# Eight PSUM banks in one tile and the remainder's steps reordered, in a six-layer cross network

## The chip, the cores and the metric

The kernel runs on one core of one Trainium2 chip. The metric is the device time of one execution in microseconds (us). The core has five engines that work off their own queues in order and wait for each other through semaphores: TensorE (PE in the profile; PEld are its weight loads), VectorE (DVE), ScalarE (ACT), GpSimd (POOL) and SyncE (SP). SP computes nothing here; it issues most of the transfers (DMA). Matmul results land in PSUM, eight banks of 512 fp32 columns by 128 partitions; all else lies in SBUF, 128 partitions wide.

## The reference

```python
B, F, D, L = 4096, 26, 16, 6
Din = min(F * D, 1024)          # 416
# x0: B x Din, ws: L x Din x Din, bs: L x Din, all bfloat16
def reference(x0, ws, bs):
    x = x0
    for l in range(ws.shape[0]):
        x = x0 * (x @ ws[l] + bs[l]) + x
    return x
```

Each of the six layers is a product of a 4096x416 matrix with a 416x416 one, then a bias, an elementwise product with the input, and an elementwise sum.

## The kernel before, in words

**Layout.** For layers 0 to 4, features lie on partitions and the 4096 batch rows on columns. 416 features are three blocks of 128 (k or m = 0, 1, 2) and a remainder of 32. The three blocks are in XM[i], with i = 0 for the input and two more for the running x. The remainder is packed into XR[i]: its 32 features for four groups of 512 batch rows lie one below the other on 128 partitions. The batch is cut into two halves s = 0, 1 of 2048, each into four groups g of 512 columns. The weights are in WM (the 384 main input rows of each layer), WR (the 32 remainder rows, repeated four times down the partitions) and WD (the remainder's own 32x32 block, laid out so that one matmul handles one group).

**Loads.** Eight transposing transfers (load_x0t, L78), all issued by SP, bring the input's main part into XM[0], 512 batch rows at a time. The remainder comes in rows of 64 bytes into xrem[s] (load_xrem, L83); x0_rem(s) then makes the packed layout from it on VectorE: 32x32 block transposes into xrt[s] (L145), a strided copy into XR[0] (L147), and two copies that put the upper 64 partitions into the lower 64 of XRx[s] and the other way round (L149), so that a remainder matmul can use either half of the rows of the array. WR of layer 0 is loaded early; the loads of WR for layers 1 to 5 (load_wr, L86) stand on SP behind the eight input transposes. fill_wd(0, 1) and fill_wd(1, L) copy the remainder blocks from WR to WD on GpSimd (L120); the second call waits for those later loads.

**Layer 0** is first_layer(s), for s = 0 and then s = 1. PE first multiplies the main blocks (function full, L206) for the first 1024 columns and the three output blocks m, into PSUM tiles pa[0] to pa[2]; then come the remainder rows (function row, L213) that close these sums; then pb[0] to pb[2] for the other 1024 columns. ew_main evicts each PSUM tile with ScalarE, which adds the bias (L154), then multiplies with the input (L155) and adds x (L156) on VectorE. The remainder's own output is made by rem_pair (mm_rem, L180 and L185; ew_rem, L160 to L162) after both halves.

**Layers 1 to 4** do the same in tiles of 2048 columns by 128 features (mm_full, L168; mm_row, L174), each in two PSUM tiles of two banks.

**The last layer** turns the product round, so that batch rows lie on partitions and the result needs no transpose: quads q = 0 to 7 of four blocks of 128 rows each, 416 columns per block. Two quads make a round: mm_q_full (L301) for the first two blocks, then mm_q_rows for both quads (remainder L309, bias by a row of ones L313), then the other blocks. ew_pair evicts two blocks at once (L322 to L325). In the last round, six of the eight blocks are evicted one by one by ew_single (L332 to L335); the output of the last block but one is issued from ScalarE's queue.

**Order.** The kernel sets manual_schedule, so each engine runs its instructions in the order in which the program text issues them; tiles from pools add the semaphores. PSUM comes from one pool of four tiles of two banks.

Of the kernel before, what the change touches and what calls it, by code (L numbers as in the profile page):

```python
# [10 lines left out]
ALU = mybir.AluOpType  # L11
# [5 lines left out]
def kernel(  # L17
# [23 lines left out]
    tpool = ctx.enter_context(tc.tile_pool(name="tpool", bufs=4))  # L41
    opool = ctx.enter_context(tc.tile_pool(name="opool", bufs=10))
    psum = ctx.enter_context(tc.tile_pool(name="psum", bufs=4, space=bass.MemoryType.PSUM))
# [37 lines left out]
    def load_xrem(eng, s):  # L81
        with nc.allow_non_contiguous_dma(reason="64B row segments"):
            eng.dma_start(xrem[s][:], x0[SW * s:SW * s + SW, NK * P:D].rearrange("(p t) r -> p t r", t=16))  # L83
# [15 lines left out]
    load_xrem(nc.scalar, 0)  # L99
    nc.scalar.activation(dz[:, 1:2], dz[:, 0:1], ACT.Identity, bias=dz[:, 0:1], scale=1.0)  # L100
    for g in range(1, NG):
        load_x0t(0, g)
        nc.vector.tensor_copy(WR[32 * g:32 * g + 32, 0, :], WR[0:32, 0, :])  # L103
    load_x0t(1, 0)
    load_xrem(nc.sync, 1)
    for g in range(1, NG):
        load_x0t(1, g)
# [17 lines left out]
    wps = psum.tile([P, CW], FP32, tag="ps", name="wps")  # L125

    def pe_filler(n, cols):
        for i in range(n):
            nc.tensor.matmul(wps[:, 0:cols], lhsT=warm[:, 0:P], rhs=warm[:, 0:cols], start=True, stop=True)  # L129
# [4 lines left out]
    def bias_setup():  # L134
        pb = psum.tile([P, 4, 8], BF16, tag="ps", name="pb")
        for m in range(NK):
            nc.tensor.transpose(pb[:, m, 0:L], bsb[0:L, 128 * m:128 * m + 128], ident[0:L, 0:L])
        for g in range(NG):
            nc.tensor.transpose(pb[32 * g:32 * g + 32, 3, 0:L], bsb[0:L, NK * P:D], ident[0:L, 0:L], tile_position=(0, 32 * g))
        nc.vector.tensor_copy(bM[:], pb[:, 0:NK, 0:L])  # L140
        nc.vector.tensor_copy(bR[:], pb[:, 3, 0:L])


    def x0_rem(s):
        nc.vector.transpose(out=xrt[s][:], in_=xrem[s][:])  # L145
        xr = XR[0][:, CW * s:CW * s + CW]
        nc.vector.tensor_copy(xr.rearrange("p (j t) -> p j t", t=16), xrt[s][:].rearrange("p t j -> p j t"))  # L147
        for a in range(2):
            nc.vector.tensor_copy(XRx[s][64 * a:64 * a + 64, :], XR[0][64 - 64 * a:128 - 64 * a, CW * s:CW * s + CW])  # L149

    def ew_main(l, s, m, h, pt, cur, nxt):
        c0 = col0(s, 2 * h)
        t = tpool.tile([P, 2 * CW], BF16, name="t")
        nc.scalar.activation(t[:], pt[:].rearrange("p a b -> p (a b)"), ACT.Identity, bias=bM[:, m, l:l + 1], scale=1.0)  # L154
        nc.vector.tensor_tensor(out=t[:], in0=t[:], in1=XM[0][:, m, c0:c0 + 2 * CW], op=ALU.mult)  # L155
        nc.vector.tensor_tensor(out=nxt[:, m, c0:c0 + 2 * CW], in0=t[:], in1=cur[:, m, c0:c0 + 2 * CW], op=ALU.add)  # L156
# [7 lines left out]
    def mm_full(l, s, m, g, pts, cur, first, last):  # L164
        c0 = col0(s, g)
        for k in range(NK):
            for q in range(4):
                nc.tensor.matmul(pts[g // 2][32 * q:32 * q + 32, g % 2, :], lhsT=WM[:, l, k, 128 * m + 32 * q:128 * m + 32 * q + 32],  # L168
                                 rhs=cur[:, k, c0:c0 + CW], start=(first and k == 0), stop=(last and k == NK - 1),
                                 tile_position=(0, 32 * q))  # L170

    def mm_row(l, s, m, pts, curR, first, last):
        for g in range(NG):
            nc.tensor.matmul(pts[g // 2][:, g % 2, :], lhsT=WR[32 * g:32 * g + 32, l, 128 * m:128 * m + 128],  # L174
                             rhs=curR[32 * g:32 * g + 32, CW * s:CW * s + CW],
                             start=first, stop=last, tile_position=(32 * g, 0))

    def mm_rem(l, s, pr, cur, curR):
        for g in range(NG):
            nc.tensor.matmul(pr[32 * g:32 * g + 32, :], lhsT=WD[:, l, g, :], rhs=curR[:, CW * s:CW * s + CW],  # L180
                             start=True, stop=False, tile_position=(0, 32 * g))
        for k in range(NK):
            for g in range(NG):
                c0 = col0(s, g)
                nc.tensor.matmul(pr[32 * g:32 * g + 32, :], lhsT=WM[:, l, k, NK * P:D], rhs=cur[:, k, c0:c0 + CW],  # L185
                      start=False, stop=(k == NK - 1), tile_position=(0, 32 * g))

    def new_pts():
        return [psum.tile([P, 2, CW], FP32, tag="ps", name=f"pt{h}") for h in range(2)]
# [7 lines left out]
    def first_layer(s):  # L197
        cur, nxt = XM[0], XM[1]

        def new_pt(m):  # L200
            return psum.tile([P, 2, CW], FP32, tag="ps", name=f"ph{m}")

        def full(pt, m, h, gl, first, last):
            c0 = col0(s, 2 * h + gl)
            for k in range(NK):
                nc.tensor.matmul(pt[:, gl, :], lhsT=WM[:, 0, k, 128 * m:128 * m + 128], rhs=cur[:, k, c0:c0 + CW],  # L206
                                 start=(first and k == 0), stop=(last and k == NK - 1))

        def row(pt, m, h, swapped, first):
            for gl in range(2):  # L210
                r0 = 32 * ((2 * h + gl + 2 * swapped) % 4)
                src = XRx[s][r0:r0 + 32, :] if swapped else XR[0][r0:r0 + 32, CW * s:CW * s + CW]
                nc.tensor.matmul(pt[:, gl, :], lhsT=WR[r0:r0 + 32, 0, 128 * m:128 * m + 128], rhs=src,  # L213
                                 start=first, stop=(not first), tile_position=(r0, 0))

        pa = [new_pt(m) for m in range(NK)]
        for gl in range(2):
            for m in range(NK):
                full(pa[m], m, 0, gl, True, False)
        pb = [new_pt(0)]  # L220
        row(pa[0], 0, 0, 0, False)
        row(pa[1], 1, 0, 1, False)
        row(pa[2], 2, 0, 0, False)
        row(pb[0], 0, 1, 0, True)
        for m in range(NK):
            ew_main(0, s, m, 0, pa[m], cur, nxt)
        for gl in range(2):
            full(pb[0], 0, 1, gl, False, True)
        ew_main(0, s, 0, 1, pb[0], cur, nxt)
        for m in range(1, NK):  # L230
            pb.append(new_pt(m))
            for gl in range(2):
                full(pb[m], m, 1, gl, True, False)
        row(pb[1], 1, 1, 0, False)
        row(pb[2], 2, 1, 1, False)
        for m in range(1, NK):
            ew_main(0, s, m, 1, pb[m], cur, nxt)
# [3 lines left out]
    x0_rem(0)  # L241
    first_layer(0)
    x0_rem(1)
    first_layer(1)

    def rem_pair(l, cur, curR, nxtR, feeds_last):
        pr2 = psum.tile([P, 2, CW], FP32, tag="ps", name="pr2")
# [9 lines left out]
    rem_pair(0, XM[0], XR[0], XR[1], False)  # L257
# [40 lines left out]
    def mm_q_full(q, py, gs, first):  # L298
        for g in gs:
            for k in range(NK):  # L300
                nc.tensor.matmul(py[g // 2][:, g % 2, 0:D], lhsT=cur[:, k, q_cols(q, g)], rhs=WM[:, l, k, :],  # L301
                                 start=(first and k == 0), stop=((not first) and k == NK - 1))


    def mm_q_rows(q, pys):
        for a in range(2):
            s, i = quads[q + a]
            for g in range(NG):
                nc.tensor.matmul(pys[a][g // 2][:, g % 2, 0:D], lhsT=curR[32 * g:32 * g + 32, CW * s + 128 * i:CW * s + 128 * i + 128],  # L309
                                 rhs=WR[32 * g:32 * g + 32, l, :], start=(a == 1 or g >= 2), stop=False, tile_position=(32 * g, 0))  # L310
        for a in range(2):
            for g in range(NG):
                nc.tensor.matmul(pys[a][g // 2][:, g % 2, 0:D], lhsT=ones[32 * g:32 * g + 1, :],  # L313
                                 rhs=bLr[32 * g:32 * g + 1, :], start=False, stop=(a == 0 and g < 2), tile_position=(32 * g, 0))
# [12 lines left out]
    def ew_single(q, g, py, eng):  # L327
# [6 lines left out]
        nc.vector.tensor_tensor(out=o[:, 0, :], in0=t[:, 0:D], in1=XLrows[:, b, :], op=ALU.add)  # L334
        return lambda: eng.dma_start(out_v[:, b, :], o[:, 0, :])  # L335

    for q in range(0, NQ, 2):
        last = q + 2 == NQ
# [3 lines left out]
        mm_q_rows(q, py)  # L342
        ew_pair(q, 0, py[0])
        if not last:
            mm_q_full(q, py[0], (2, 3), False)
            ew_pair(q, 1, py[0])
            for h in range(2):
                mm_q_full(q + 1, py[1], (2 * h, 2 * h + 1), False)
                ew_pair(q + 1, h, py[1])
        else:  # L350
            for a, g in ((0, 2), (0, 3), (1, 0), (1, 1), (1, 2), (1, 3)):
                mm_q_full(q + a, py[a], (g,), False)
                ew_single(q + a, g, py[a], nc.scalar if (a, g) == (1, 2) else nc.sync)()
# [30 lines left out]
```

## Time and profile before

| | us |
|---|---|
| median of 3 runs | 137.73 (136.46 to 138.05) |
| the profiled execution | 136.52 |
| its span, first to last instruction | 134.4 |
| PE, DVE, ACT, POOL busy in it | 122.7, 111.0, 83.9, 6.0 |
| mean granted TensorE clock | 0.998 |

The profile describes one execution. Its page gives busy time per engine, the tenths of busy time in 40 slices of the span, the chain of work that ended last, and the costliest groups of instructions. The trace behind it gives each instruction with its start, and for idle time the event that ended it (after the arrow). A line number is that of the kernel's text. "issue" stands for waiting that the profile shows no cause for. A matmul is listed with its whole length, some 380 ns, but matmuls follow each other closer than that, so the pace of PE is read from starts.

The largest groups by time:

```profile
L168 PE MATMUL pt<-XM,WM 128*32 128x512 bf16 x1152 | 65.2, 379 | 0.0
L154 ACT ACTIVATE t<-pt,bM 128x1024 bf16<-128x1024 f32 x48 | 49.6, 1115 | 20.7 <-PE pt L174 20.7
L155 DVE TENSOR_TENSOR t<-t,XM 128x1024 bf16<-128x1024 bf16 x60 | 41.7, 695 | 7.0 <-ACT t L154 7.0
L156 DVE TENSOR_TENSOR XM<-t,XM 128x1024 bf16<-128x1024 bf16 x60 | 41.7, 696 | 3.5
```

### The profile page before, as it was taken

How to read it: one execution, taken by the hardware profiler on the slowest of the kernel's cores; microseconds unless marked ns; L12 is line 12 of the kernel's file. 1: busy time of each engine (PE TensorE's matmuls, PEld its weight loads, DVE VectorE, ACT ScalarE, POOL GpSimd, SP SyncE). 2: the span in 40 equal slices, each digit the busy share in tenths (PEclk: the TensorE clock that was granted, in tenths of full speed). 3: DMA queues.
4: the chain of work that ended last, by engine and by line, in shares of the span. 5: the costliest groups of instructions: out<-in, count | busy, mean ns of one | idle time of the engine just before them, and what ended most of it. 6: DMA issues, size and time to landing. Idle time of an engine off the chain costs nothing.

```text
span 134.4 us, 3926 instructions
## 1 busy us (share of the span) xinstructions
PE 122.7 (91%) x1681; PEld 54.8 (41%) x1683; DVE 111.0 (83%) x194; ACT 83.9 (62%) x91; POOL 6.0 (4%) x18
## 2 busy tenths in 40 slices
PE   6979984998999999999999999999999999999640
PEld 2323331443444444444444434444444444544310
DVE  1254996998897988999898989898989999999852
ACT  1306833883939495859577856849584966766640
POOL 4110000400000000000000000000003200000000
PEclk9999999999999999999999999999999999999999
DMA  3999999999930000000000000000598999965541
GB/s 97 247 225 189 163 228 236 304 330 333 335 97 0 0 5 2 5 0 5 0 5 0 5 0 5 0 5 0 106 133 185 170 203 188 274 222 185 180 147 56
DMA packets 41989, 16.37 MB, mean 122 GB/s; under 512 B 30794, under 2 KB 41972, under 8 KB 41972
## 3 DMA queue, kind: packets, MB, share of 16 engines
q1 hardware_dynamic: 39304, 15.53, 50.9%
q10 hardware_dynamic: 2668, 0.59, 2.3%
q8 instruction: 13, 0.21, 0.6%
q14 instruction: 4, 0.03, 0.1%
HBM read 6.15 MB, written 3.41 MB: 71 GB/s over the span
## 4 chain that ended last, share of the span: by engine, by line
PE 70%; SPq 15%; DVE 5%; DMA 4%; ACT 2%; issue 1%; ACTq 0%
PE pt L168 45%; PE pt L301 12%; SPq L78 12%; PE pt L174 5%; DMA WM<-in_ws_dram 4%; PE pr L185 4%; DVE XM L156 2%; ACT t L332 2%; DVE t L155 1%; PE pt L309 1%; SPq L86 1%; PE pr L180 1%; SPq L74 1%; PE pt L313 1%; DVE t L333 1%
## 5 line engine op out<-in xcount | busy, mean ns | idle before, releaser
L168 PE MATMUL pt<-XM,WM 128*32 128x512 bf16 x1152 | 65.2, 379 | 0.0
L154 ACT ACTIVATE t<-pt,bM 128x1024 bf16<-128x1024 f32 x48 | 49.6, 1115 | 20.7 <-PE pt L174 20.7
L155 DVE TENSOR_TENSOR t<-t,XM 128x1024 bf16<-128x1024 bf16 x60 | 41.7, 695 | 7.0 <-ACT t L154 7.0
L156 DVE TENSOR_TENSOR XM<-t,XM 128x1024 bf16<-128x1024 bf16 x60 | 41.7, 696 | 3.5
L168 PEld LDWEIGHTS <-WM 128*32 128x32 bf16 x1152 | 29.7, 97 | 33.8 <-issue 5.1
L154 ACT ACTIVATE t<-ph,bM 128x1024 bf16<-128x1024 f32 x12 | 12.5, 1113 | 12.5 <-PE ph L213 12.5
L301 PE MATMUL pt<-WM,XM 128*128 128x416 bf16 x96 | 18.2, 339 | 1.8 <-ACT t L332 1.8
L206 PE MATMUL ph<-XM,WM 128*128 128x512 bf16 x70 | 16.3, 379 | 1.2 <-DMA XM<-in_x_dram 1.1
L322 ACT CAST t<-pt 128x832 bf16<-128x832 f32 x13 | 11.1, 852 | 5.8 <-PE pt L313 3.1
L301 PEld LDWEIGHTS <-XM 128*128 128x128 bf16 x96 | 9.0, 98 | 10.8 <-issue 3.9
L206 PEld LDWEIGHTS <-WM 128*128 128x128 bf16 x72 | 6.8, 98 | 10.1 <-issue 2.7
L185 PE MATMUL pr<-XM,WM 128*32 128x512 bf16 x120 | 8.2, 379 | 0.0
L324 DVE TENSOR_TENSOR o<-t,XLrows 128x832 bf16<-128x832 bf16 x13 | 7.7, 592 | 0.6
L323 DVE TENSOR_TENSOR t<-t,X0rows 128x832 bf16<-128x832 bf16 x13 | 7.6, 586 | 0.4 <-ACT t L322 0.3
L174 PE MATMUL pt<-XR,WR 32*128 32x512 bf16 x96 | 7.3, 379 | 0.6 <-DVE XR L162 0.6
L160 ACT ACTIVATE t<-pr,bR 128x512 bf16<-128x512 f32 x10 | 6.3, 686 | 2.1 <-PE pr L185 2.1
L129 PE MATMUL wps<-warm 128*128 128x512 bf16 (+1 forms) x12 | 4.2, 518 | 1.2 <-DVE warm L89 1.2
L254 POOL COPY XLrows<-scrR 128x512 bf16<-128x512 bf16 x2 | 1.7, 891 | 77.5 <-DMA scrR<-XR 77.5
L332 ACT CAST t<-pt 128x416 bf16<-128x416 f32 x6 | 3.0, 506 | 3.0 <-DVE o L334 1.4
L162 DVE TENSOR_TENSOR XR<-t,XR 128x512 bf16<-128x512 bf16 x10 | 4.3, 425 | 0.8
L103 DVE COPY WR<-WR 32x416 bf16<-32x416 bf16 x3 | 0.8, 259 | 4.6 <-DMA WR<-in_ws_dram 4.6
L185 PEld LDWEIGHTS <-WM 128*32 128x32 bf16 x120 | 3.2, 97 | 3.2
(36 smaller groups left out, 38.3 us busy)
## 6 DMA issues: line engine op xcount, KB each, us to landing
X0rows<-in_x_dram SPq DMA_DIRECT2D x4, 832.0 KB, 10.5
out_dram<-o SPq DMA_DIRECT2D x13, 208.0 KB, 2.2
WM<-in_ws_dram SPq DMA_DIRECT2D x5, 312.0 KB
WR<-in_ws_dram SPq DMA_DIRECT2D x4, 130.0 KB, 4.8
out_dram<-o SPq DMA_DIRECT2D x5, 104.0 KB, 1.7
WM<-in_ws_dram ACTq DMA_DIRECT2D x1, 312.0 KB, 3.5
XM<-in_x_dram SPq DMA_TRANSPOSE x8, 4.8
xrem<-in_x_dram ACTq DMA_DIRECT2D x1, 128.0 KB
```

The costliest lines, as they stand in the source:

```text
L78: nc.sync.dma_start_transpose(out=XM[0][:, :, c0:c0 + CW], in_=x0[c0:c0 + CW, 0:NK * P])
L154: nc.scalar.activation(t[:], pt[:].rearrange("p a b -> p (a b)"), ACT.Identity, bias=bM[:, m, l:l + 1], scale=1.0)
L155: nc.vector.tensor_tensor(out=t[:], in0=t[:], in1=XM[0][:, m, c0:c0 + 2 * CW], op=ALU.mult)
L156: nc.vector.tensor_tensor(out=nxt[:, m, c0:c0 + 2 * CW], in0=t[:], in1=cur[:, m, c0:c0 + 2 * CW], op=ALU.add)
L168: nc.tensor.matmul(pts[g // 2][32 * q:32 * q + 32, g % 2, :], lhsT=WM[:, l, k, 128 * m + 32 * q:128 * m + 32 * q + 32], rhs=cur[:, k, c0:c ...
L174: nc.tensor.matmul(pts[g // 2][:, g % 2, :], lhsT=WR[32 * g:32 * g + 32, l, 128 * m:128 * m + 128], rhs=curR[32 * g:32 * g + 32, CW * s:CW ...
L185: nc.tensor.matmul(pr[32 * g:32 * g + 32, :], lhsT=WM[:, l, k, NK * P:D], rhs=cur[:, k, c0:c0 + CW], start=False, stop=(k == NK - 1), tile ...
L206: nc.tensor.matmul(pt[:, gl, :], lhsT=WM[:, 0, k, 128 * m:128 * m + 128], rhs=cur[:, k, c0:c0 + CW], start=(first and k == 0), stop=(last ...
L301: nc.tensor.matmul(py[g // 2][:, g % 2, 0:D], lhsT=cur[:, k, q_cols(q, g)], rhs=WM[:, l, k, :], start=(first and k == 0), stop=((not first ...
L322: nc.scalar.copy(tv, py[h][:, :, 0:D])
L323: nc.vector.tensor_tensor(out=tv, in0=tv, in1=X0rows[:, b0:b0 + 5:4, :], op=ALU.mult)
L324: nc.vector.tensor_tensor(out=o[:], in0=tv, in1=XLrows[:, b0:b0 + 5:4, :], op=ALU.add)
```

## The change

- PSUM is one tile PS of eight banks; two_banks() hands out pairs of banks in turn. The buffers t go from four to six.
- The bias is brought onto partitions by matmuls with the identity into fp32, not by transposes into bf16.
- load_xrem and x0_rem take a range of partitions, and x0_rem an engine for its copies. The first half's remainder is loaded in two parts: partitions 0 to 63 from ScalarE's queue at the head, 64 to 127 from SP ahead of the fourth input transpose. The second half's load moves behind one more transpose.
- x0_rem(0, 0, 64) stays at the head, on VectorE. x0_rem(0, 64, 128) stands in first_layer(0), its block transposes on VectorE and its copies on GpSimd. x0_rem(1) moves into first_layer(0), ahead of the elementwise work on its second 1024 columns.
- In first_layer(0) all remainder rows of pb come after all main products of pb. In first_layer(1) the main products go block by block; the first layer's remainder product (rem_first) comes ahead of the last two evictions of main blocks.
- In the last layer, the last two quads are opened one at a time, all eight of their blocks are evicted singly, the sum of each block is issued after the product of the next, and all outputs go from SP.
- skip_group_check is passed to the matmuls.

```diff
-    tpool = ctx.enter_context(tc.tile_pool(name="tpool", bufs=4))
+    tpool = ctx.enter_context(tc.tile_pool(name="tpool", bufs=6))
     opool = ctx.enter_context(tc.tile_pool(name="opool", bufs=10))
-    psum = ctx.enter_context(tc.tile_pool(name="psum", bufs=4, space=bass.MemoryType.PSUM))
+    psum = ctx.enter_context(tc.tile_pool(name="psum", bufs=1, space=bass.MemoryType.PSUM))
...
-    def load_xrem(eng, s):
+    def load_xrem(eng, s, p0, p1):
         with nc.allow_non_contiguous_dma(reason="64B row segments"):
-            eng.dma_start(xrem[s][:], x0[SW * s:SW * s + SW, NK * P:D].rearrange("(p t) r -> p t r", t=16))
+            eng.dma_start(xrem[s][p0:p1], x0[SW * s + 16 * p0:SW * s + 16 * p1, NK * P:D].rearrange("(p t) r -> p t r", t=16))
...
-    load_xrem(nc.scalar, 0)
+    load_xrem(nc.scalar, 0, 0, 64)
     nc.scalar.activation(dz[:, 1:2], dz[:, 0:1], ACT.Identity, bias=dz[:, 0:1], scale=1.0)
     for g in range(1, NG):
-        load_x0t(0, g)
         nc.vector.tensor_copy(WR[32 * g:32 * g + 32, 0, :], WR[0:32, 0, :])
+    load_x0t(0, 1)
+    load_x0t(0, 2)
+    load_xrem(nc.sync, 0, 64, 128)
+    load_x0t(0, 3)
     load_x0t(1, 0)
-    load_xrem(nc.sync, 1)
-    for g in range(1, NG):
-        load_x0t(1, g)
+    load_x0t(1, 1)
+    load_xrem(nc.sync, 1, 0, 128)
+    load_x0t(1, 2)
+    load_x0t(1, 3)
     load_wm(nc.sync, 1)
     for g in range(NG):
         load_wr(nc.sync, g, 1, L)
...
     fill_wd(0, 1)
     fill_wd(1, L)
...
-    wps = psum.tile([P, CW], FP32, tag="ps", name="wps")
+    PS = psum.tile([P, 8, CW], FP32)
+    turn = [0]
+
+    def two_banks():
+        i = 2 * (turn[0] % 4)
+        turn[0] += 1
+        return PS[:, i:i + 2, :]
...
-        pb = psum.tile([P, 4, 8], BF16, tag="ps", name="pb")
+        pb = PS[:, 7, 0:32].rearrange("p (a b) -> p a b", a=4)
         for m in range(NK):
-            nc.tensor.transpose(pb[:, m, 0:L], bsb[0:L, 128 * m:128 * m + 128], ident[0:L, 0:L])
+            nc.tensor.matmul(pb[:, m, 0:L], lhsT=bsb[0:L, 128 * m:128 * m + 128], rhs=ident[0:L, 0:L], start=True, stop=True,
+                             skip_group_check=True)
...
-    def x0_rem(s):
-        nc.vector.transpose(out=xrt[s][:], in_=xrem[s][:])
-        xr = XR[0][:, CW * s:CW * s + CW]
-        nc.vector.tensor_copy(xr.rearrange("p (j t) -> p j t", t=16), xrt[s][:].rearrange("p t j -> p j t"))
-        for a in range(2):
-            nc.vector.tensor_copy(XRx[s][64 * a:64 * a + 64, :], XR[0][64 - 64 * a:128 - 64 * a, CW * s:CW * s + CW])
+    def x0_rem(s, p0, p1, eng):
+        nc.vector.transpose(out=xrt[s][p0:p1], in_=xrem[s][p0:p1])
+        eng.tensor_copy(XR[0][p0:p1, CW * s:CW * s + CW].rearrange("p (j t) -> p j t", t=16),
+                              xrt[s][p0:p1].rearrange("p t j -> p j t"))
+        for a in range(p0, p1, 64):
+            eng.tensor_copy(XRx[s][64 - a:128 - a, :], XR[0][a:a + 64, CW * s:CW * s + CW])
...
+        pa = [two_banks() for m in range(NK)]
+        if s == 0:
+            for gl in range(2):
+                for m in range(NK):
+                    full(pa[m], m, 0, gl, True, False)
+        else:
             for m in range(NK):
-                full(pa[m], m, 0, gl, True, False)
-        pb = [new_pt(0)]
+                for gl in range(2):
+                    full(pa[m], m, 0, gl, True, False)
+        pb = [two_banks()]
         row(pa[0], 0, 0, 0, False)
         row(pa[1], 1, 0, 1, False)
         row(pa[2], 2, 0, 0, False)
-        row(pb[0], 0, 1, 0, True)
+        if s == 1:
+            row(pb[0], 0, 1, 0, True)
+        if s == 0:
+            x0_rem(0, 64, 128, nc.gpsimd)
         for m in range(NK):
             ew_main(0, s, m, 0, pa[m], cur, nxt)
         for gl in range(2):
-            full(pb[0], 0, 1, gl, False, True)
-        ew_main(0, s, 0, 1, pb[0], cur, nxt)
+            full(pb[0], 0, 1, gl, s == 0, s == 1)
+        if s == 1:
+            ew_main(0, s, 0, 1, pb[0], cur, nxt)
         for m in range(1, NK):
-            pb.append(new_pt(m))
+            pb.append(two_banks())
             for gl in range(2):
                 full(pb[m], m, 1, gl, True, False)
-        row(pb[1], 1, 1, 0, False)
-        row(pb[2], 2, 1, 1, False)
-        for m in range(1, NK):
-            ew_main(0, s, m, 1, pb[m], cur, nxt)
+        if s == 0:
+            row(pb[0], 0, 1, 0, False)
+            row(pb[2], 2, 1, 1, False)
+            row(pb[1], 1, 1, 0, False)
+            x0_rem(1, 0, 128, nc.vector)
+            for m in range(NK):
+                ew_main(0, s, m, 1, pb[m], cur, nxt)
+        else:
+            row(pb[1], 1, 1, 0, False)
+            row(pb[2], 2, 1, 1, False)
+            rem_first(pb)
 
     bias_setup()
     pe_filler(1, CW)
-    x0_rem(0)
-    first_layer(0)
-    x0_rem(1)
-    first_layer(1)
+    x0_rem(0, 0, 64, nc.vector)
...
+    def rem_first(pb):
+        pr2 = two_banks()
+        for s in range(NS):
+            mm_rem(0, s, pr2[:, s, :], XM[0], XR[0])
+        for s in range(NS):
+            ew_rem(0, s, pr2[:, s, :], XR[0], XR[1])
+            ew_main(0, 1, 1 + s, 1, pb[1 + s], XM[0], XM[1])
+
+    first_layer(0)
+    first_layer(1)
...
-    for q in range(0, NQ, 2):
-        last = q + 2 == NQ
+
+        def close():
+            nc.vector.tensor_tensor(out=o[:, 0, :], in0=t[:, 0:D], in1=XLrows[:, b, :], op=ALU.add)
+            nc.sync.dma_start(out_v[:, b, :], o[:, 0, :])
+
+        return close
+
+    for q in range(0, NQ - 2, 2):
         py = [new_pts()]
         mm_q_full(q, py[0], (0, 1), True)
         py.append(new_pts())
-        mm_q_rows(q, py)
+        mm_q_rows((q, q + 1), py, q)
         ew_pair(q, 0, py[0])
-        if not last:
-            mm_q_full(q, py[0], (2, 3), False)
-            ew_pair(q, 1, py[0])
-            for h in range(2):
-                mm_q_full(q + 1, py[1], (2 * h, 2 * h + 1), False)
-                ew_pair(q + 1, h, py[1])
-        else:
-            for a, g in ((0, 2), (0, 3), (1, 0), (1, 1), (1, 2), (1, 3)):
-                mm_q_full(q + a, py[a], (g,), False)
-                ew_single(q + a, g, py[a], nc.scalar if (a, g) == (1, 2) else nc.sync)()
+        mm_q_full(q, py[0], (2, 3), False)
+        ew_pair(q, 1, py[0])
+        for h in range(2):
+            mm_q_full(q + 1, py[1], (2 * h, 2 * h + 1), False)
+            ew_pair(q + 1, h, py[1])
+    pending = []
+    for q in range(NQ - 2, NQ):
+        py = new_pts()
+        mm_q_rows((q,), (py,), None)
+        for g in range(NG):
+            mm_q_full(q, py, (g,), False)
+            close = ew_single(q, g, py)
+            if pending:
+                pending.pop()()
+            pending.append(close)
+    pending.pop()()
...
```

## The prediction

> **What bounds the kernel now.** I read the busy table first, then the chain that ended last, then the table of waits, and then the order of instructions in the first 42 us and the last 12 us. The busy table and the digits of the 40 slices say who carries the time (columns: busy us, share of the span, instructions; then tenths of each slice):
>
> ```profile
> PE 122.7 (91%) x1681; PEld 54.8 (41%) x1683; DVE 111.0 (83%) x194; ACT 83.9 (62%) x91; POOL 6.0 (4%) x18
> ...
> PE   6979984998999999999999999999999999999640
> ```
>
> TensorE (PE) is full from about slice 10 to slice 36. A change can win only in the holes of the first ten slices (0 to 33 us) and in the last four, and any new hole on PE comes straight out as time. GpSimd (POOL) looks free with 4%, and that is the trap to look into. The waits show the holes (us in total, times, longest):
>
> ```profile
> POOL WD L120 <- DMA WR<-in_ws_dram: 20.7, 5, 15.9
> ...
> PE ph L213 <- DVE XR L147: 2.0, 1, 2.0
> ...
> PE pt L301 <- ACT t L332: 1.8, 3, 0.6
> ...
> ACT t L332 <- DVE o L334: 1.4, 1, 1.4
> ...
> PE pt L174 <- DVE XR L162: 0.6, 1, 0.6
> ```
>
> PE waits 2.0 us for the second half's remainder (x0_rem(1), queued on VectorE behind six elementwise pairs), 0.6 us for the first layer's new remainder, and 1.8 us in the last round for ScalarE's evictions. POOL itself waits 20.7 us for the remainder weights of the later layers. Its instructions in order of time (start, length, idle before):
>
> ```profile
> 6.09 1.06 POOL L120 COPY WD<-WR 32x32 bf16<-32x32 bf16 x4 [3.97 <-DMA WR<-in_ws_dram]
> 23.07 0.31 POOL L120 COPY WD<-WR 32x160 bf16<-32x160 bf16 x1 [15.91 <-DMA WR<-in_ws_dram]
> 23.76 0.45 POOL L120 COPY WD<-WR 32x160 bf16<-32x160 bf16 x1 [0.38 <-DMA WR<-in_ws_dram]
> 24.42 0.52 POOL L120 COPY WD<-WR 32x160 bf16<-32x160 bf16 x1 [0.21 <-DMA WR<-in_ws_dram]
> 25.12 0.54 POOL L120 COPY WD<-WR 32x160 bf16<-32x160 bf16 x1 [0.19 <-DMA WR<-in_ws_dram]
> 103.12 1.73 POOL L254 COPY XLrows<-scrR 128x512 bf16<-128x512 bf16 x2 [77.46 <-DMA scrR<-XR]
> ```
>
> From 7.15 to 25.66 us POOL stands at, or works off, the four copies of fill_wd(1, L). They wait for loads that the DMA-issuing engine (SP) starts only at 18.46 us, behind all eight input transposes. Nothing behind those copies in POOL's order can start before 25.66 us.
>
> **The change part by part.**
>
> *The remainder on POOL.* For the first half s = 0, x0_rem is split at partition 64. The lower part stays on VectorE at the head. Of the upper part only the 32x32 transposes stay on VectorE; the strided copy into XR[0] and the copy into XRx[0] go to POOL, and they are issued after fill_wd(1, L). So they stand directly behind the copy that ended at 25.66 us. Who waits: the first-layer rows of pb, whose operand is just that upper half (XR[0] partitions 64 to 127, and XRx[0] partitions 0 to 63). PE reaches these rows where it ran the s = 0 rows before, at 15.36 us:
>
> ```profile
> 1.19 3.83 PE L129 MATMUL wps<-warm 128*128 128x256 bf16 x11 [1.19 <-DVE warm L89]
> ...
> 15.36 0.39 PE L213 MATMUL ph<-XR,WR 32*128 32x512 bf16 x2
> ...
> 15.69 4.06 PE L206 MATMUL ph<-XM,WM 128*128 128x512 bf16 x18
> ```
>
> Behind them on PE's queue stands everything else, the whole second half of the batch included. When are they released? SP has one more issue ahead of the WR loads, the second part of xrem[0]: the whole load took 0.67 us to issue, half of it 0.33 by size (ends: 0, if the loads are paced by the traffic, and 0.67). So the last WD copy ends at 25.66 + 0.33 = 25.99. The trace shows no such copy on POOL; the nearest row is L254, 128x512, 0.72 and 1.06 us, mean 0.89. Two of them, one waiting for the other: 25.99 + 1.78 + two gaps of 0.04 = 27.85. The rows of pb[0] can go after the first copy, at 26.9, the other four at 27.85.
>
> From there PE's work up to the next common point, the rows of layer 1 (L174 at 32.37 before), is, start to start in the timeline of before: four rows 0.33, 18 matmuls 3.99, eight rows 0.55, 18 matmuls 3.99, four rows 0.32, the remainder product 1.74, 48 matmuls of layer 1 2.70. The sum is 13.62, so 27.85 + 13.62 = 41.47, which is 9.10 us later than 32.37. (Before, the same 13.62 from 15.36 and 3.39 us of waiting made 32.37; those waits are swallowed by the long one and are not to be taken off again.) ScalarE's evictions don't lengthen this: pb[0] of s = 0 leaves at 27.3 to 28.4, pb[1] by 29.5, pb[2] by 30.6, each before PE wants its banks back (29.5, 30.9, 32.7).
>
> *PE's rate after the stop.* The stop is 11.5 us, against a longest idle of 2.02 us on PE before, after which 18 matmuls still ran in 3.99 us, 0.22 each. The only longer rest in the trace is the one ahead of the program: there eleven fillers (nine of 512 columns) took 3.83 us, some 0.38 to 0.43 each, half the rate. If a stop of 11.5 us brings that back, nine matmuls at 0.43 in place of 0.22 cost 1.8 us; ends 0 (as after 2.02 us) and 2.3 (slow from 1.19 to the first fast matmul at 5.78, half of it lost). I take 1.8, since 11.5 us is nearer to the unused engine than to 2 us. The granted clock reads 1.00 in the filler stretch too, so that row can't show this effect. The Trainium skill, "TensorE: Matmul & The Clock Gate", Part 1: The HAM clock gate, says that the array falls to half rate after an idle window of about 3.4 us and needs about as long a busy one to return; by it the sum would have 1.7 us here, an estimate. The fillers agree with the half rate; no idle of that length is in the trace to try the rest.
>
> *What is hidden under that stop.* xrem[1] is loaded one transpose later: issue about 10.50 + 2.93 + 0.33 = 13.8, landing 4.3 later at 18.1, and VectorE transposes and copies it by 20.1 (0.70 + 0.59 + 0.59 and gaps), ahead of the s = 0 elementwise work of the second column half. That work waits for evictions after 27 us, so it costs nothing here. VectorE's transpose of the upper part waits for a load issued at about 6.7 and landed near 11.0; it is done by 11.8, before the first elementwise operation at 12.40. The remainder product ahead of the last evictions removes the 0.6 us wait at L174 (its first XR[1] half is ready at 39.9, PE asks at 41.5): already in the sum. The bias by matmuls in fp32 in place of seven transposes (0.17 us each) ends well before VectorE's next wait at 8.54: nothing.
>
> *Eight banks as one tile, six t buffers.* Banks still turn in pairs, and in the built program as many matmuls wait for ScalarE (83) as before. In the middle PE is at nine tenths and waits for nobody, so nothing is gained: 0. What it allows is in the tail.
>
> *The last two rounds.* Before, ScalarE's copy of one bank and the next matmul in the same two-bank tile took turns: three waits of 0.59. Then ScalarE stood 1.4 us at an output issue. Both go. But VectorE is late there already, and it sets the end:
>
> ```profile
> 124.05 0.59 DVE L324 TENSOR_TENSOR o<-t,XLrows 128x832 bf16<-128x832 bf16 x1
> ...
> 131.41 0.38 DVE L334 TENSOR_TENSOR o<-t,XLrows 128x416 bf16<-128x416 bf16 x1
> ```
>
> At 124.64 VectorE ends the last round but two. Now eight single blocks follow instead of one pair and six singles. A single costs 0.70 (126.11, 126.80, 127.50 are successive starts): 124.64 + 8 x 0.70 = 130.24, against 131.79. PE would deliver the last block at 127.6 and ScalarE evict it by 128.1, so they keep ahead. Gain 1.55, ends 0 and 2.0. The SP issues (0.38 each) keep up with 0.70.
>
> Sum on the profiled execution: 136.52 (span 134.4 and 2.1 around it) + 9.10 + 1.8 - 1.55 = 145.9. That execution lies 1.2 us under the median 137.73 of the three; I add half of that: 146.5.
>
> **Rivals.**
> - *POOL does not hold it (the faster side).* If the WD copies were over by about 13.5 us, the pb rows would start at 15.36 and the three waits of 3.39 us would really go: 136.52 - 3.39 - 1.55 = 131.6, with the 0.6 for the median 132.2. The point from which it decides: every microsecond by which POOL is free before 25.66 comes off. For it: the copies are only 1.8 us of work. Against it: SP starts those loads at 18.46 and the change moves none of them forward. Chance 0.04.
> - *No loss of rate after the stop:* 146.5 - 1.8 = 144.7. For it: no loss after 2.02 us of idle. Chance 0.18.
> - *The strided copy is dear on POOL.* VectorE's strided copy L147 took 0.59, its plain copy L149 0.29: twice. The same ratio on POOL adds 0.93: 147.4. Chance 0.20.
> - *One tile serialises.* If each matmul group waited for evictions of other banks, sixty evictions of 1.1 us would come onto PE, over 200 us. Against it: the count of waits. Chance 0.01.
> - *Something gives it back within 1%,* such as loads that come some 9 us earlier than they can by the issue times. Chance 0.02.
>
> My forecast has 0.55. Low end: no loss of rate (-1.8), both copies at 0.72 and no SP delay (-0.7), the profiled level rather than the median (-0.6): 143.4. High end: 2.3 for the rate (+0.5), SP 0.67 (+0.3), copies at 1.06 (+0.3), strided copy dear (+0.9), all of the median (+0.6): 149.1. About 1%, the spread of the three runs, is what a measurement here can tell from no change: faster 0.04, within 1% 0.02, slower 0.94.
>
> **What would show it.** In the profile after: PE idle for about 11 us before the pb rows, released by POOL's XR copy; POOL's XR and XRx copies at about 26 to 28 us, right behind the WD copies; matmuls of the second half 0.43 apart for some 4 us, then 0.22; the rows of layer 1 near 43; no waits on ScalarE in the last two rounds, and VectorE the last engine. The forecast is wrong if POOL's two copies stand before 20 us, or if the hole on PE is filled.

## The result, and the profile after

| us | before | after |
|---|---|---|
| median of four runs | 137.12 (136.46 to 138.05) | 147.06 (145.06 to 147.58) |
| the profiled execution | 136.52 | 147.55 |
| its span | 134.4 | 145.7 |
| mean granted TensorE clock in it | 0.998 | 0.946 |

The kernel is slower, by a ratio of 1.063 (95% interval 1.047 to 1.079). The ratio leaves out two runs of the changed kernel that lie more than 1.5% above its fastest, the profiled one among them; so it is smaller than that of the medians in the table.

The busy table and the 40 slices of the changed kernel:

```profile
PE 126.2 (87%) x1683; PEld 55.3 (38%) x1683; DVE 110.7 (76%) x196; ACT 83.9 (58%) x92; POOL 6.7 (5%) x20
...
PE   6999200199999999999999999999999999999960
...
PEclk9999985557999999999999999999999999999997
```

TensorE now stands still from slice 5 to slice 8, and the clock granted to it is halved in slices 7 to 9 (of 3.64 us each), that is into the work that follows the stop. The table of waits (us in total, times, longest) names who released TensorE, and what GpSimd itself stood for:

```profile
POOL WD L124 <- DMA WR<-in_ws_dram: 23.1, 5, 18.3
...
PE PS L222 <- POOL XR L158: 13.4, 1, 13.4
```

GpSimd's instructions in order of time (start, length, idle before) show why the copies of the remainder come so late: they stand behind four copies of remainder weights.

```profile
25.34 0.31 POOL L124 COPY WD<-WR 32x160 bf16<-32x160 bf16 x1 [18.29 <-DMA WR<-in_ws_dram]
...
27.26 0.32 POOL L124 COPY WD<-WR 32x160 bf16<-32x160 bf16 x1 [0.30 <-DMA WR<-in_ws_dram]
27.64 1.03 POOL L158 COPY XR<-xrt 64x512 bf16<-64x512 bf16 x1
28.73 0.61 POOL L161 COPY XRx<-XR 64x512 bf16<-64x512 bf16 x1
```

TensorE in order of time, from the stop to the first rows of layer 1:

```profile
28.72 0.61 PE L222 MATMUL PS<-XR,WR 32*128 32x512 bf16 x2 [13.36 <-POOL XR L158]
...
29.93 6.25 PE L215 MATMUL PS<-XM,WM 128*128 128x512 bf16 x18
...
36.66 4.06 PE L215 MATMUL PS<-XM,WM 128*128 128x512 bf16 x18
...
45.41 0.61 PE L186 MATMUL PS<-XR,WR 32*128 32x512 bf16 x8
```

The wait of 13.36 us ends at 28.72, as L158 ends. The eighteen matmuls that follow take 6.25 us where the next eighteen of the same shape take 4.06. Two stretches of the same trace show the clock (length, then busy time of PE, PEld, DVE, ACT, POOL, then granted clock, DMA share, GB/s):

```profile
20.00:25.00 5.00, 0.00 (x0) 0.00 (x0) 0.14 (x1) 0.00 (x0) 0.00 (x0) 0.58 1.16 236
33.00:35.00 2.00, 2.00 (x8) 0.75 (x7) 1.55 (x3) 0.00 (x0) 0.00 (x0) 0.65 1.12 334
```

The clock falls while TensorE rests, some 5.5 us after it stopped, and is still low when it has been at work for 4 us. It is back at about 34.4.

The rows of layer 1 come at 45.41 us, 13.04 later than before (32.37). From there to the third round of the last layer nothing changes: those rounds too start 13.04 later (118.20 before, 131.24 after). The end is shorter. VectorE's last block, in the timeline of all engines:

```profile
137.09 0.59 DVE L358 TENSOR_TENSOR o<-t,XLrows 128x832 bf16<-128x832 bf16 x1
...
141.75 0.65 DVE L370 TENSOR_TENSOR o<-t,XLrows 128x416 bf16<-128x416 bf16 x2
```

VectorE ends at 142.40, which is 96.99 us behind the rows of layer 1; before it was 99.42 (131.79 less 32.37). What follows VectorE's end grew from 2.6 to 3.3 us. The spans differ by 13.04 - 2.43 + 0.7 = 11.3 us, and that is 145.7 less 134.4.

### The profile page after: what moved, and what is told of

It reads as the page before. It is cut to its first block, busy times and chain, and to the rows that moved or that the text cites. A ratio compares the mean times of both kernels' runs of the same rounds, so it can differ in the third digit from the quotient of the medians.

```text
span 145.7 us, 3943 instructions
## 1 busy us (share of the span) xinstructions
PE 126.2 (87%) x1683; PEld 55.3 (38%) x1683; DVE 110.7 (76%) x196; ACT 83.9 (58%) x92; POOL 6.7 (5%) x20
## 4 chain that ended last, share of the span: by engine, by line
PE 75%; SPq 13%; DMA 4%; POOL 2%; DVE 1%; issue 1%; ACT 0%; DVEq 0%; POOLq 0%
PE PS L180 44%; SPq L78 11%; PE PS L332 11%; PE PS L215 7%; PE PS L186 4%; PE PS L197 4%; DMA WR<-in_ws_dram 4%; PE PS L192 2%; PE PS L341 1%; PE PS L222 1%; PE PS L346 1%; SPq L83 1%; DVE t L367 1%; POOL XR L158 1%; SPq L86 1%
## 5 line engine op out<-in xcount | busy, mean ns | idle before, releaser
L166 ACT ACTIVATE t<-PS,bM 128x1024 bf16<-128x1024 f32 x60 | 62.1, 1114 | 47.1 <-PE PS L222 25.8
L180 PE MATMUL PS<-XM,WM 128*32 128x512 bf16 x1152 | 65.2, 379 | 0.0
L180 PEld LDWEIGHTS <-WM 128*32 128x32 bf16 x1152 | 29.7, 97 | 33.8 <-issue 5.1
L215 PE MATMUL PS<-XM,WM 128*128 128x512 bf16 x72 | 18.9, 423 | 0.0
L332 PE MATMUL PS<-WM,XM 128*128 128x416 bf16 x96 | 17.9, 340 | 0.0
L222 PE MATMUL PS<-XR,WR 32*128 32x512 bf16 x16 | 2.8, 434 | 13.4 <-POOL XR L158 13.4
L356 ACT CAST t<-PS 128x832 bf16<-128x832 f32 x12 | 10.2, 852 | 5.0 <-PE PS L332 2.5
L197 PE MATMUL PS<-XM,WM 128*32 128x512 bf16 x120 | 8.2, 379 | 0.0
L172 ACT ACTIVATE t<-PS,bR 128x512 bf16<-128x512 f32 x10 | 6.8, 694 | 1.4 <-PE PS L197 1.4
L186 PE MATMUL PS<-XR,WR 32*128 32x512 bf16 x96 | 7.3, 379 | 0.0
L139 PE MATMUL PS<-warm 128*128 128x512 bf16 (+1 forms) x12 | 5.1, 594 | 1.2 <-DVE warm L89 1.2
L366 ACT CAST t<-PS 128x416 bf16<-128x416 f32 x8 | 4.0, 505 | 1.0 <-PE PS L332 0.8
```

Source lines behind the costliest of these rows:

```text
L166: nc.scalar.activation(t[:], pt.rearrange("p a b -> p (a b)"), ACT.Identity, bias=bM[:, m, l:l + 1], scale=1.0)
L356: nc.scalar.copy(tv, py[h][:, :, 0:D])
```

## The experiments

The theory is that the order of GpSimd holds the two copies back, and that the long stop it makes costs TensorE its rate as well. The rivals are that GpSimd is a poor engine for these copies wherever they stand, that the stop costs its length alone, that the single PSUM tile does harm, and that the new order at the end does. The first four kernels ran on one chip beside 13 runs of the kernel before (137.69, 136.68 to 137.96).

**The weight copies behind the remainder's.** The changed kernel with one line moved:

```diff
     fill_wd(0, 1)
-    fill_wd(1, L)
...
     first_layer(0)
+    fill_wd(1, L)
     first_layer(1)
```

> The changed kernel with one call moved: fill_wd(1, L) behind first_layer(0), so that GpSimd's two remainder copies stand ahead of the four WD copies. Theory (the WD copies hold the remainder copies, and PE with them): the 13.4 us wait of PE for GpSimd's XR copy goes, the three waits of 3.4 us of before go too, and the tail keeps its gain of about 1.7 us (2.4 on VectorE, 0.7 given back at the last outputs): 136.5 - 3.4 + 0.3 - 1.7 = 131.7 us, with a granted clock of 1.0 throughout. Rival (the moved loads or the one PSUM tile cost the time): stays above 144 us.

Measured: 132.07 (131.84 to 132.72), ratio 0.961 (0.955 to 0.966). One line turns the loss of 6% into a gain of 4%. GpSimd in order of time:

```profile
11.10 1.03 POOL L157 COPY XR<-xrt 64x512 bf16<-64x512 bf16 x1 [4.05 <-DVE xrt L156]
12.19 0.96 POOL L160 COPY XRx<-XR 64x512 bf16<-64x512 bf16 x1
24.96 2.99 POOL L124 COPY WD<-WR 32x160 bf16<-32x160 bf16 x4 [11.80 <-DMA WR<-in_ws_dram]
```

The same two copies end at 13.15 instead of 29.34. The weight copies still wait for their loads until 24.96, and now hold nobody.

**The remainder's copies on VectorE.**

```diff
-            x0_rem(0, 64, 128, nc.gpsimd)
+            x0_rem(0, 64, 128, nc.vector)
```

> The changed kernel with the same two copies on VectorE instead of GpSimd; GpSimd's order as it is. Theory (GpSimd's order, not GpSimd's speed): as with the WD copies moved, 131.7 us, within 0.5 of it, since VectorE has 1.2 us of idle time at that place for 0.59 + 0.29 us of copies. Rival (copying on GpSimd is dear in itself, slow or by sharing SBUF with VectorE): faster than the variant with GpSimd's copies ahead by over 0.5 us. Rival (loads or PSUM tile): above 144 us.

Measured: 131.93 (131.66 to 132.06), ratio 0.960 (0.955 to 0.965), the same as with the line moved. GpSimd's speed is not the matter; its order is. Both kernels keep the loads in the changed kernel's order and its single PSUM tile, so these did not make the loss. The rows of layer 1 start at 29.99 us, so the place of two copies that last 1.64 us together costs 15.4 us at that point (45.41 less 29.99), and 15.1 by the medians.

**Work for TensorE during the stop.** The changed kernel with 58 matmuls on spare data ahead of the rows that wait; their results are overwritten:

```diff
         if s == 0:
+            for i in range(58):
+                nc.tensor.matmul(PS[:, 5, :], lhsT=warm[:, 0:P], rhs=warm[:], start=True, stop=True, skip_group_check=True)
             row(pb[0], 0, 1, 0, False)
```

> The changed kernel with 58 more matmuls of 512 columns on the constant tile into an idle bank, issued on PE ahead of the rows that wait for GpSimd; nothing else changes and their result is not used. They take some 12.5 us of the 13.4 us stop. Theory (after the stop PE runs at half rate for some 5 us): the first 18 matmuls of the second half take 4.0 us instead of 6.2, granted clock 1.0, so 147.1 - 2.3 = 144.8 us. Rival (no loss of rate; the second half starts slowly for another reason, such as its weights or loads): 147 us, 18 matmuls still in about 6 us.

Measured: 144.21 (143.48 to 144.57), ratio 1.049 (1.043 to 1.055), with a mean granted clock of 1.000. Its four executions have 0.996 to 1.000, those of the changed kernel 0.935 to 0.964. TensorE in order of time:

```profile
14.96 12.68 PE L254 MATMUL PS<-warm 128*128 128x512 bf16 x58
27.87 0.39 PE L222 MATMUL PS<-XR,WR 32*128 32x512 bf16 x2 [0.23 <-POOL XR L158]
...
28.87 4.06 PE L215 MATMUL PS<-XM,WM 128*128 128x512 bf16 x18
```

The eighteen matmuls are back at 4.06 us. From the release to the rows of layer 1 it is 14.28 us (27.87 to 42.15), against 16.69 in the changed kernel (28.72 to 45.41): the lost rate is worth 2.4 us. The other 0.85 between the two is an earlier release. In this execution the weight copies ended 0.85 us sooner, although SP began to issue their loads 1.03 us later (20.64 against 19.61). The fillers concern TensorE alone, so when the loads land is not set by their issue alone; it differs from one profiled execution to another.

**The new order at the end alone.** The kernel before, with its PSUM pool, and the last two rounds of the changed kernel:

```diff
-    for q in range(0, NQ, 2):
+    for q in range(0, NQ - 2, 2):
...
+    for q in range(NQ - 2, NQ):
+        py = new_pts()
+        mm_q_rows((q,), (py,), None)
+        for g in range(NG):
+            mm_q_full(q, py, (g,), False)
+            close = ew_single(q, g, py)
+            if pending:
+                pending.pop()()
+            pending.append(close)
+    pending.pop()()
```

> The kernel before with the changed last two rounds alone (opened one at a time, all eight blocks single, sum issued after the next product, outputs on SP), PSUM still a pool of four two-bank tiles, head as before. Theory (the tail's gain needs the waits between the two banks of a tile gone): PE still waits about 0.59 us four times, some 1.8 us per two blocks, VectorE ends within 0.5 us of before: 136.5 to 137.5 us. Rival (the order of the tail alone brings the gain): 1.7 us less than before, 134.8 to 135.4 us.

Measured: 138.17 (137.09 to 138.44), ratio 1.003 (1.000 to 1.007). By itself the order gains nothing: with two-bank tiles the trace has four waits of 0.59 us of TensorE for ScalarE's copies, where each quad goes on from one bank of a tile to the other.

The next four kernels ran on another chip, beside seven runs of the kernel before (137.64, 136.41 to 138.0). All start from the kernel with the copies on VectorE (131.93).

**Four two-bank tiles in place of the single tile.**

```diff
-    PS = psum.tile([P, 8, CW], FP32)
-    turn = [0]
     def two_banks():
-        i = 2 * (turn[0] % 4)
-        turn[0] += 1
-        return PS[:, i:i + 2, :]
+        return psum.tile([P, 2, CW], FP32, tag="ps", name="pq")[:]
```

(with `bufs=4` in the pool, and tiles from it for the first fillers and the bias)

> The variant with the copies on VectorE (131.9 us), with PSUM again a pool of four two-bank tiles. Theory (the one tile matters only in the last two rounds, where a matmul no longer waits for the copy of the other bank): head and middle as in that variant; four waits of 0.59 us for ScalarE return, the last two rounds grow by 2.2 us (2.9 on VectorE, 0.7 less at the outputs): 134.1 us. Rival (the one tile costs or gains nothing anywhere): 131.9 us. Rival (the one tile costs something in the middle by coarser waits): below 131.5 us.

Measured: 134.52 (134.49 to 135.07), ratio 0.981 (0.975 to 0.986). The median is 2.6 us above that of the single tile (131.93, on the first chip), and the spans differ by 2.5. TensorE in the last round but one:

```profile
121.50 1.22 PE L329 MATMUL pq<-WM,XM 128*128 128x416 bf16 x6 [0.59 <-ACT t L363]
123.31 0.69 PE L329 MATMUL pq<-WM,XM 128*128 128x416 bf16 x3 [0.59 <-ACT t L363]
```

With the single tile, twelve such matmuls follow each other there in 2.28 us without a wait. From the rows of layer 1 to the start of the last round but one it takes 89.91 us with four tiles and 89.92 with one, so the difference lies in the last two rounds: in the middle the single tile is worth nothing. VectorE ends at 129.70 instead of 126.99.

**The sum right behind its product.**

```diff
-            if pending:
-                pending.pop()()
-            pending.append(close)
-    pending.pop()()
+            close()
```

> The variant with the copies on VectorE (131.9 us), with each block's sum issued right behind its own product in the last two rounds, as before. Theory (the prediction's 0.70 us per block came from that order; issued one block apart a block costs 0.57): eight blocks grow by 0.13 us each, 1.0 in all: 132.9 us. Rival (the order of sum and product doesn't matter, the 0.57 comes from ScalarE no longer being waited for): 131.9 us.

Measured: 132.34 (132.16 to 132.6), ratio 0.964 (0.959 to 0.969). VectorE needs 5.65 us for the eight blocks instead of 4.81, 0.70 each instead of 0.60. Only 0.4 of the 0.84 reaches the time, since 2.75 us follow VectorE's end instead of 3.2: the last two outputs become ready 0.70 us apart and no longer 0.28, so SP's last issue ends 0.35 us behind VectorE instead of 0.77.

**The first half's remainder loaded whole.** One load from ScalarE's queue at the head, as before the change:

```diff
-    load_xrem(nc.scalar, 0, 0, 64)
+    load_xrem(nc.scalar, 0, 0, 128)
...
-    load_xrem(nc.sync, 0, 64, 128)
...
-        if s == 0:
-            x0_rem(0, 64, 128, nc.vector)
...
-    x0_rem(0, 0, 64, nc.vector)
+    x0_rem(0, 0, 128, nc.vector)
```

> The variant with the copies on VectorE (131.9 us), with the first half's remainder loaded in one piece from ScalarE's queue and prepared whole at the head, as before. Theory (the second part on SP holds up the fourth input transpose by 0.7 us and with it PE's 0.66 us wait and all that SP issues later): the wait at 12.2 us goes and everything behind SP comes 0.6 us earlier: 131.3 us. Rival (the split pays: the whole load lands later and PE waits for the first rows): 132 us or more, with a wait of PE for XR near 10.2 us.

Measured: 131.56 (131.28 to 131.68), ratio 0.958 (0.953 to 0.963). The load in two parts wins nothing here. With it, in the kernel of 131.93, TensorE waits 0.66 us for an input transpose that SP issues later; with the whole load it waits 0.33 us for an earlier one. In the other kernels with two parts and no stop that wait is 0.40 to 0.59 us, and with four PSUM tiles it is absent. The two medians come from two chips and the ranges touch (131.28 to 131.68 and 131.66 to 132.06), so what the whole load gains, 0.4 us by the medians, is not pinned to this wait.

**VectorE's order at the first layer's remainder.** As the last kernel, with the remainder's product and sum of s = 0 ahead of those of pb[0], and the very last output issued from ScalarE's queue:

```diff
-            ew_main(0, s, 0, 1, pb[0], cur, nxt)
+            close = ew_open(0, s, 0, 1, pb[0], cur, nxt)
...
-            nc.sync.dma_start(out_v[:, b, :], o[:, 0, :])
+            (nc.scalar if (q, g) == (NQ - 1, NG - 1) else nc.sync).dma_start(out_v[:, b, :], o[:, 0, :])
```

(`ew_open` is the eviction by ScalarE; it returns VectorE's two operations, which the remainder's product then calls behind its own.)

> The variant with the whole load, and two more edits: VectorE does the first remainder product of layer 0 ahead of the main block pb[0] of the second half (ScalarE's order as it is), and the last output is issued from ScalarE's queue. Theory: PE's 0.60 us wait at the rows of layer 1 goes, the last output is issued 0.4 us earlier: 131.3 - 0.6 - 0.4 = 130.3 us. Rival (VectorE's queue only moves the wait to the next one, the output's landing sets the end): 131.3 us.

Measured: 131.28 (131.08 to 131.52), ratio 0.956 (0.950 to 0.962). The first edit did what it should: the rows of layer 1 start at 29.05 without a wait, 0.55 us earlier than in the kernel of 131.56. The second gained nothing, so the expected 130.3 was missed: 3.35 us follow VectorE's end (126.05, span 129.4), against 3.1 in that kernel.

Three last kernels ran on a third chip, beside seven runs of the kernel before (136.62, 136.37 to 138.07).

**The kernel before, a second profile.**

> The kernel before, unchanged, for a second profile. Its executions fall near 136.6 or near 137.7 us, the higher ones with a granted clock near 0.985. Theory: the higher ones lose PE's rate for some us in the first 30 us (at the start, or after the 2 us wait for the second half's remainder), which a profile of such an execution shows as matmuls over 0.22 us apart there. Rival: the 1.1 us lie in loads or in the outputs, with the matmuls at 0.22 us throughout.

Measured: 137.82, with a mean granted clock of 0.986. In stretches of time (columns as above):

```profile
22.00:23.00 1.00, 0.77 (x8) 0.11 (x5) 0.25 (x1) 0.90 (x1) 0.00 (x0) 0.77 1.16 206
23.00:24.00 1.00, 1.00 (x5) 0.38 (x4) 0.73 (x1) 1.00 (x2) 0.51 (x2) 0.50 1.14 231
24.00:25.00 1.00, 1.00 (x4) 0.37 (x3) 0.98 (x2) 1.00 (x2) 0.81 (x3) 0.50 1.11 331
25.00:26.00 1.00, 1.00 (x3) 0.30 (x2) 0.96 (x2) 0.36 (x2) 0.61 (x1) 0.53 1.12 329
26.00:27.00 1.00, 0.95 (x5) 0.49 (x5) 0.96 (x3) 0.97 (x1) 0.00 (x0) 1.00 1.12 331
```

After the same wait of 2.02 us (TensorE starts again at 21.68) the clock falls to 0.50 for some 3.4 us, and eighteen matmuls take 5.39 us start to start instead of 3.99. The rows of layer 1 come at 33.64 instead of 32.37. So behind this wait the rate is lost in some executions and not in others. Three profiles have the wait, and one of them the loss (the new order at the end alone has the wait and reads 1.00); in the eight profiles of kernels that have neither this wait nor the stop the clock reads 1.00 from 20 to 30 us. It fits the times: of the 31 runs of the kernel before, twelve lie between 136.3 and 136.9, like the first profiled one, and nineteen between 137.5 and 138.1, like this one. The mean granted clock, on record for 27 of them, parts the two groups without exception: 0.976 to 0.987 in the seventeen slower ones, 0.995 to 0.999 in the ten faster. A mean does not say where in the execution the clock fell; that is shown for the one profile.

**The best version with its last output on SP.** The kernel of 131.28, its second edit taken back:

```diff
-            (nc.scalar if (q, g) == (NQ - 1, NG - 1) else nc.sync).dma_start(out_v[:, b, :], o[:, 0, :])
+            nc.sync.dma_start(out_v[:, b, :], o[:, 0, :])
```

> The best variant so far (131.28 us) with the last output on SP again. Theory (an output from ScalarE's queue lands 0.5 us later than one from SP, which takes back the 0.4 us of the earlier issue): 131.0 to 131.3 us, not slower. Rival (the ScalarE queue did help): 131.6 us.

Measured: 131.07 (130.87 to 131.28), ratio 0.958 (0.951 to 0.964), the lowest median of all, though not set apart from 131.28. It beats both kernels.

**The head alone.** The kernel with the copies on VectorE, its single PSUM tile kept, and the last rounds as they were before the change:

```diff
-    for q in range(0, NQ - 2, 2):
+    for q in range(0, NQ, 2):
+        last = q + 2 == NQ
...
+            for a, g in ((0, 2), (0, 3), (1, 0), (1, 1), (1, 2), (1, 3)):
+                mm_q_full(q + a, py[a], (g,), False)
+                ew_single(q + a, g, py[a], nc.scalar if (a, g) == (1, 2) else nc.sync)()
```

> The variant with the copies on VectorE (131.9 us), with the last round as before: one pair and six single blocks, sum behind product, the last output but one from ScalarE's queue; one PSUM tile. Theory (VectorE ends 1.7 us later, of which 1.1 for the last eviction standing behind that output on ScalarE's queue, and the outputs at the end cost 0.6 less): 133.0 us. Rival (with the bank waits gone the old order is as good): 131.9 us.

Measured: 133.61 (132.99 to 134.16), ratio 0.977 (0.971 to 0.983). VectorE ends at 129.00 instead of 126.99, and VectorE again waits 0.99 us for the last eviction, because ScalarE stands 2.60 us at an output that it issues. So of the 5.8 us between the kernel before and the one with the copies on VectorE (137.7 to 131.9), some 1.7 belong to the end (133.6 to 131.9) and the rest, about 4, to the head. That split takes medians from two chips and depends on which of the two groups above the kernel before falls in: beside its own seven runs (136.62) the head alone is worth 3.0. By the traces the rows of layer 1 come at 29.93, which is 2.4 us earlier than in the first profile of before and 3.7 earlier than in the second. The new end pays only with the single tile, as the new order at the end alone showed.

## Why the prediction was right

The forecast was 146.5 by the runs and 145.9 on the profiled execution; these measured 147.06 and 147.55. Sign, cause and place are those predicted. That the median came within 0.6 us is in part luck: on the profiled execution the forecast is 1.65 us too low. Four terms had the wrong size: the weight copies' end and the rate, both too small, and two at the end of the kernel that nearly cancel (1.73 us gained in all, where 1.55 were forecast).

*Where the copies stand: right.* The two copies follow the last weight copy with nothing between, TensorE waits for the first of them, and it works off everything else behind that wait. The rival "POOL does not hold it" was false here. It was put at 132.2, and the two kernels in which GpSimd does not hold the rows measured 132.07 and 131.93, but the parts of that price did not hold. It took off three waits of 3.39 us. With the copies on VectorE the rows of layer 1 came only 2.38 us earlier than before (29.99 against 32.37): TensorE waited 0.66 us for a transpose, and still 0.60 for the first layer's new remainder. The 0.6 added for the median covered most of that difference.

*The end of the weight copies: 1.6 us too early.* They were put at 25.99 and ended at 27.58. Two readings failed. SP's half-size load was put at 0.33 by its size, but took the same 0.67 us to issue as the whole one; with the input transposes behind it, SP came to the weight loads 1.15 us later (19.61 against 18.46), and not 0.33. And the loads were taken to land as long after their issue as before; the first copy came 5.73 us behind the first issue instead of 4.61. That second part is no property of the change: in the kernel with the fillers it was 3.73. The bounds put to this term, 0 to 0.67, came from issue times alone and should have had the spread of the landings too, for which one trace of before gave only one value.

*The copies themselves: right in sum, wrong in each.* Two at 0.89 were forecast, and 1.03 and 0.61 came. The strided copy does cost more than the plain one, as that rival had it, by 1.7 times; but the plain one is cheaper than the row it was taken from, so nothing is added.

*TensorE's rate: right in kind, too small.* 1.8 us were forecast, 2.4 measured, and the fillers show the cause, because they give the rate back without moving the release by more than its spread. The end put at 2.3 was nearer than the value taken. The rival "no loss of rate" had one thing for it, the wait of 2.02 us without a loss. That was one execution: the second profile of the same kernel shows a loss of 1.4 us behind the same wait. The prediction also said that the granted clock can't show this effect, because it reads 1.00 beside the slow fillers at the start. Behind a stop it does show it, with 0.50.

The Trainium skill, "TensorE: Matmul & The Clock Gate", Part 1: The HAM clock gate, has the array at half rate after an idle window of about 3.4 us, and counts by windows that do not start with the kernel's own work. The half rate agrees with the 0.50. Windows whose phase varies would fit one wait that costs nothing in one execution and 1.4 us in another, which no run here shows directly. But the 2.02 us, with the 0.23 that follows some matmuls later, are shorter than such a window, and still the clock fell; for the length that suffices the measurement stands against the page.

*The middle: right.* It was put at nothing, and is 0.0 by the trace of the changed kernel and 0.01 us by the kernel with four tiles. The rival "one tile serialises" is false: the single tile is what takes the waits of 0.59 us away.

*The end: right in cause, too small.* No wait of TensorE for ScalarE is left in the last two rounds, and VectorE is the last engine. It gained 2.43 us and not 1.55, because a block takes 0.57 to 0.60 and not 0.70. The 0.70 was read from singles whose sum directly follows its own product; in the changed kernel another block's product lies between them, and the kernel with the sum right behind shows the 0.70 again. What the prediction missed is the cost of that order: the last two sums end 0.28 us apart, SP issues their outputs one after the other, and its last issue ends 0.80 us behind VectorE instead of 0.35. That is 0.45 of the 0.7 us given back; the rest lies between that issue and the end of the span. "SP keeps up" was true of all blocks but the last.

*Hidden under the stop: as said.* VectorE's transpose, the later load of xrem[1] and the bias by matmuls cost nothing there. Without the stop the load in two parts wins nothing, as the kernel with the whole load showed.

## What to carry to other kernels

Before work is moved to an engine that looks idle, read that engine's instructions in order of time: GpSimd was busy for 4% and could take nothing new before 25.66 us, and moving one line of its order was worth 15 us here. A stop of TensorE is to be priced at its length and the slow stretch behind it. A change that mixes several edits is worth taking apart: this one held 5.8 us of gain beneath a single misplaced call.

## What the runs showed of the hardware

Behind a wait of 2.02 us on TensorE its granted clock was halved for some 3.4 us in one execution (137.82) and stayed at 1.00 in another (136.52), with the same instructions. A stop of 13.36 us halved it some 5.5 us after the stop began, and it was back some 5.7 us after work resumed (28.72 to about 34.4).

A product of VectorE and a copy of GpSimd took longer where the two engines worked at the same time. VectorE's instructions in order of time, in the kernel with the weight copies moved; the first product lies beside GpSimd's two copies (11.10 to 13.15), the second behind them:

```profile
11.68 1.01 DVE L166 TENSOR_TENSOR t<-t,XM 128x1024 bf16<-128x1024 bf16 x1 [0.71 <-ACT t L165]
...
13.63 0.68 DVE L166 TENSOR_TENSOR t<-t,XM 128x1024 bf16<-128x1024 bf16 x1
```

The one takes 1.01 us and the other 0.68. GpSimd's plain 64x512 copy took 0.96 there, and 0.61 in the changed kernel, where VectorE rested; its strided copy, beside VectorE for less than half its time, took 1.03 in both.

A VectorE operation on 128x416 elements that needs the result of the one ahead started 0.40 us behind its start, and one that does not, 0.28 to 0.29: that is the 0.70 and the 0.57 per block (126.11, 126.51 and 126.80 in the kernel before; 138.45, 138.74 and 139.02 in the changed one).

A remainder load of 64 partitions took SP 0.67 us to issue; those of 128 partitions took 0.59 to 0.67.
